# Loads of the later pairs moved to SyncE's queue in single rows, and two more pairs transposed by the DMA crossbar

## The chip, the cores and the metric

The kernel runs on one core of a Trainium2 chip. A core has a matrix engine (TensorE, PE in the profile, with its weight loads as PEld), a vector engine (VectorE, DVE), an engine for activation functions (ScalarE, ACT), a general one (GpSimd, POOL) and one that only waits and issues transfers (SyncE, SP). The transfers of all of them run on the same 16 DMA engines. The metric is the device time of one execution in microseconds (us), lower is better; several runs of the same kernel are given by their median.

## The reference

Two computations follow each other. The first is a gated linear recurrence: for each of 4 batches and 8 heads, with 768 positions t and a head size of 48,

```
state = alpha[t, :, None] * state + k[t] (outer) v[t]
y[t]  = q[t] @ state
```

The second is a two-layer network on y, read as x of 3072 rows (batch and position) by 384 (heads and their elements):

```
h   = x @ w_in            # 384 -> 2048
out = gelu_tanh(h) @ w_out  # 2048 -> 384, out is 3072 x 384 f32
```

All inputs are f32 in memory, laid out batch, head, position, element, so one head's row of one position is 48 x 4 = 192 bytes.

## The kernel before

**Tiles.** The 768 positions are cut into 6 chunks c of 128, and the 4 batches into 2 halves i. A "pair" m is one (c, i), numbered 0 to 11 with i running fastest: two units (batches) of one chunk, 128 positions by 2 batches by 8 heads by 48. Pairs 6 and 7 are chunk 3, pairs 8 to 11 are chunks 4 and 5.

**One pair.** `load` (L213) brings a strip of each of alpha (tile `a`), q, k in f32 (384 KB) and of v, cast to bf16 on the way (192 KB written). `ln` (L239, ACT) takes the logarithm of alpha, `cum` (L246, PE) sums it over positions with a triangular matrix, `exp` (L261, ACT) makes the decay b, its inverse, and the chunk's end decay. `scaled` (L276, DVE) makes q' = q b and k' = k / b (tiles `qp`, `kp`). q' and k' must then be transposed to have the head's elements on the partitions (tile `qkT`). There are two ways of doing this: `turn` and `turned` (L284, L301) with PE, 8 transposes a unit, into PSUM, and a copy out by DVE; or `turn_dma` (L308), a DMA transpose issued by SP, one for q' and one for k' of the whole pair. `attn` (L318) multiplies k' and q' per head, `mask` (L330, DVE) zeroes the upper part, `kv` (L338) and `carry` (L349) advance the state, `y` (L365) adds the state's part and the chunk's own part, `x` (L380) copies y to bf16, and x is transposed into `xT`, again by PE (`turn_x`, `turned_x`) or by SP (`turn_x_dma`, L315).

**One block** of the network is one pair's 256 rows: `layer1` (L396, 16 tiles of 3 matmuls) makes hT, `gelu` (L405, ACT) makes gT, `layer2` (L409) makes acc, `result` copies it to `ot`, and `store` (L424) sends it out through SP.

**Order.** Nothing is ordered by the hardware's own choice. `Scheduler.order` (L50) plays the kernel through on a clock of its own, with a cost for each task (the table `W`, L15), and gives each engine a fixed list. A task can start when its dependencies are done and when the buffer it takes (`BUFS`, L147) has been given back; of the tasks that could start within 60 ns of the earliest on an engine, the one with the lowest priority number goes first. A pair's tasks have numbers near 100 m; the network's tasks have 10000 and up, keep their own order, and fill what the pairs leave. ACT needs one table for ln and exp and another for gelu, so `DECAYS` (L139) says after which block's gelus each pair's ln and exp stand: those of pairs 6 and 7 both stand after block 4.

**Buffers that matter here.** Four each of `a`, `q`, `k` and six of `v`; one PSUM slot shared by `cum` and `at`; two (`yk`) shared by the PE transposes, kv, y and PE's transposes of x; four (`ff`) shared by hT and acc; four `qkT`; six `ot`.

**Queues.** In the kernel before, SP issues the first strip of alpha, all stores, and the DMA transposes, which pairs 8 to 11 use for q', k' (`TURN_QK`) and x (`TURN_X`, L146). POOL issues all other loads, in the order of `LOADS` (L143). Both issue strictly in order, and a transfer whose semaphore is not there yet holds all that stands behind it. A DMA of either queue also reuses the completion semaphore of the eighth before it on that queue, and waits for it.

Of the kernel before, what the change touches and what calls it, by code (L numbers as in the profile page):

```python
# [5 lines left out]
BF16 = mybir.dt.bfloat16  # L6
F16 = mybir.dt.float16
F32 = mybir.dt.float32
# [3 lines left out]
LN_EXP, GELU = 6, 0  # L12


W = dict(  # L15
    ln=760, exp=720, bend=170, gelu4=510, gelu2=340, table=1290,
    cum=530, t8=450, t4=225, attn=340, kv=170, inter=170, intra=205, tx=168, l1_4=655, l1_2=340, l2=655,
    qk2=910, qk1=500, ev8=650, ev4=350, mask=640, st=1400, st0=700, xc=520, xe=330, ot=540,
    ev8_act=960, ev4_act=520, xc_act=450, xe_act=450, ot_act=450,
    strip=2120, cast=1500, weight=1850, dma=2100, issue=1100, wissue=760, sp=100, store=2600, turn=1250, landed=2200, xbar_qk=1500, xbar_x=1000, first=3470, cold=500, fill=216, zero=1100,  # L20
)
LAT = {"SP": 0, "PE": 210, "ACT": 110, "DVE": 90, "POOL": 0}

# [1 line left out]
class Task:  # L25


    def __init__(self, kind, cost, prio, emit, deps=(), table=None, land=None, stream=None, xbar=0, late=0):
        self.kind, self.cost, self.prio, self.emit = kind, cost, prio, emit
        self.deps, self.takes = list(deps), []  # L30
        self.table, self.land, self.stream, self.xbar = table, land, stream, xbar
        self.late = late
        self.end = self.done = None

    def take(self, tag, *users):
# [4 lines left out]
class Scheduler:  # L40
# [9 lines left out]
    def order(self):  # L50
        free = {e: 0 for e in LAT}
        taken = {tag: [] for tag in self.bufs}
        table, wire, xbar, head, out = LN_EXP, 0, 0, 0, []
        left = {e: sorted((t for t in self.tasks if e in t.cost), key=lambda t: t.prio) for e in LAT}

        def given(tag):

            n, at = len(taken[tag]) - self.bufs[tag], 0
            for u in taken[tag][n] if n >= 0 else ():
                if u.done is None:  # L60
                    return None
                at = max(at, u.done)
            return at

        def ready(t):
            if t.stream not in (None, head):
                return None
            at = 0
            for d in t.deps:
                if d.done is None:  # L70
                    return None
                at = max(at, d.done)
            for tag, _ in t.takes:
                g = given(tag)
                if g is None:
                    return None
                at = max(at, g)
            return at

        def put(t, at, e):  # L80
            nonlocal wire, xbar
            for tag, users in t.takes:
                taken[tag].append(users)
            t.start, t.end, t.engine, t.load = at, at + t.cost[e], e, None
            free[e] = t.end
            t.done = t.end + LAT[e]
            if t.land is not None:
                wire = t.done = max(wire, t.end + W["dma"] - t.land) + t.land
            if t.kind in ("turn", "store"):
                xbar = t.done = max(xbar, t.end + W["landed"] - t.xbar) + t.xbar  # L90
                t.done += t.late
            out.append(t)

        while any(left.values()):
            best = None
            for e in LAT:
                found = []
                for t in left[e]:
                    at = ready(t)
                    if at is not None:  # L100
                        turn = W["table"] if t.table not in (None, table) else 0
                        at = max(at, free[e] + turn)
                        found.append((at, t, at - turn))
                if found:
                    window = min(f[2] for f in found) + 60
                    at, t, _ = min((f for f in found if f[2] <= window), key=lambda f: (f[1].prio, f[0]))
                    if best is None or at < best[0]:
                        best = at, e, t
            assert best is not None, "no task can go on"
            at, e, t = best  # L110
            if e == "PE" and self.fill and at < self.until and at - free[e] > 500:
                g = given("ff")
                n = int((at - max(free[e], g if g is not None else at) - 100) * 0.8 // W["fill"])
                if not free[e]:
                    n = int((at - W["zero"]) // W["cold"])
                if n > 0:
                    f = Task("fill", {"PE": n * W["fill"]}, 0, self.fill(n))
                    put(f.take("ff", f), max(free[e], g), e)
            put(t, at, e)
            if t.stream is not None:  # L120
                head += 1
            if t.table not in (None, table):
                table = t.load = t.table
            for q in t.cost:
                left[q].remove(t)
        return out
# [9 lines left out]
class _Kernel:  # L136
# [6 lines left out]
    LOADS = ("0", "1", "in 0", "in 1", "in 2", "in 3", "out 0", "out 1", "out 2", "out 3",  # L143
             "2", "3", "4", "5", "6", "7", "8", "9", "10", "11")

    TURN_QK, TURN_X = (8, 9, 10, 11), (8, 9, 10, 11)  # L146
    BUFS = dict(ca=1, yk=2, ff=4, la=3, qp=4, kp=4, b8=2, qkT=4, atm=6, x=3, ot=6, bend=8,  # L147
                a=4, q=4, k=4, v=6)

# [63 lines left out]
    def load(self, n, c, i, lo=0, hi=2):  # L213

        nc, C, H, D = self.nc, self.C, self.H, self.D
        u = self.p[c, i]

        def emit(e):
            if n not in u:
                u[n] = self.tile(n, [C, 2, H, D], BF16 if n == "v" else F32)  # L220
            src = self.src[n][2 * i + lo:2 * i + hi].rearrange("b h s d -> s (b h) d")[c * C:(c + 1) * C]
            (nc.sync if e == "SP" else nc.gpsimd).dma_start(u[n][:, lo:hi].rearrange("t b h d -> t (b h) d"), src)  # L222
        return emit

    def load_w(self, which, part):
# [203 lines left out]
    def tasks(self):  # L429
        s = self.s = Scheduler(self.BUFS, self.fill, 60000)  # L430
# [3 lines left out]
        pairs = list(self.p)  # L434


        loads, n = {}, 0

        def load(key, cost, emit):
            nonlocal n  # L440
            land = W[{"v": "cast", "w": "weight"}.get(key[0], "strip")]
            loads[key] = s.add("load", {"POOL": cost}, n, emit, land=land // 2 if key[0] != "w" and key[1] in self.SPLIT else land)
            n += 1

        def rows(m, names="aqkv"):
            for lo, hi in self.parts(m):
                for r in names:
                    load((r, m, lo), W["issue"] * (hi - lo) // 2, self.load(r, *pairs[m], lo, hi))
                    loads[r, m, hi - 1] = loads[r, m, lo]
# [6 lines left out]
        for step in self.LOADS:  # L456
            if step == "0":
                rows(0, "qkv")
            elif step.isdigit():
                rows(int(step))  # L460
            else:
                weights(*step.split())


        states, ys, xts, lns, ends = {}, {}, {}, {}, {}
        for m, (c, i) in enumerate(pairs):
            u, P = self.p[c, i], 100 * m
# [3 lines left out]
            for lo, hi in self.parts(m):  # L471
                n = hi - lo
# [10 lines left out]
                step = 1 if early else n  # L483
# [7 lines left out]
            exps[0].take("b8", *qp, *kp)  # L491
            vs, kvs, tq, cs, users = [], [], [], [], []
            if m in self.TURN_QK:
                tq = [s.add("turn", {"SP": W["turn"]}, P + 10, self.turn_dma(u, n), d, xbar=W["xbar_qk"]) for n, d in (("q", qp), ("k", kp))]
                owner, turned = tq[0], tq
            for j in range(2):
                b, o = 2 * i + j, P + 10 + 3 * j
                k = kp[j]
# [18 lines left out]
                          ms + turned + [loads["v", m, j]] + ([states[b, c - 1]] if c else []))  # L517
                xc = s.add("x", {"ACT": W["xc_act"], "DVE": W["xc"]}, P + 20 + j, self.x(u, j), [y])
                if m in self.TURN_X:
                    xe = tx = s.add("turn", {"SP": W["turn"]}, P + 22 + j, self.turn_x_dma(u, j, c, b), [xc], xbar=W["xbar_x"])  # L520
                else:
                    tx = s.add("tx", {"PE": W["tx"]}, P + 22 + j, self.turn_x(u, j), [xc])
                    xe = s.add("xe", {"DVE": W["xe"]}, P + 22 + j, self.turned_x(u, j, c, b), [tx])
                    tx.take("yk", xe)
# [4 lines left out]
                xts[c, b], ys[b, c] = xe, y  # L529
                vs.append(y)  # L530
                if c < NCH - 1:
                    kv = s.add("kv", {"PE": W["kv"]}, P + 30 + j, self.kv(u, j), [k, loads["v", m, j]])
                    st = states[b, c] = s.add("st", {"DVE": W["st" if c else "st0"]}, P + 30 + j, self.carry(u, j, c, b),
                                              [kv, be[j]] + ([states[b, c - 1], ys[b, c - 1]] if c else []))
                    kv.take("yk", st)
                    vs.append(kv)
                    kvs.append(kv)
                    cs.append(st)
# [106 lines left out]
```

## Time and profile before

| what | us |
|---|---|
| median of 3 runs | 188.83 (188.6 to 188.84) |
| the profiled execution, its own time | 188.71 |
| span of the profile | 186.9 |
| PE busy | 176.7 |
| ACT busy | 131.8 |
| DVE busy | 104.0 |
| POOL busy | 63.8 |

The span runs from the first to the last instruction of the profile; 1.8 us of the profiled execution's time lie outside it. Busy times are unions of instructions, so an engine that is 95% busy can only be passed by work that makes it shorter. Of the views, the page gives the shares, the chain that ended last gives what each stretch waited for, the stage table gives the busy time of each engine between two moments, the timelines give single instructions with the idle time before them in brackets, and the list of DMA issues gives the time from an issue to its landing.

### The profile page before, as it was taken

The page shows a single profiled execution, that of the slowest core. Times are in us where ns is not written, and L with a number is a line of the kernel's source. Part 1 is how long each engine was busy: PE and PEld are TensorE (multiplying, and loading weights), DVE is VectorE, ACT ScalarE, POOL GpSimd, SP SyncE. Part 2 cuts the span into 40 slices and gives each one's busy share as a digit, 9 for nine tenths or more (in the row PEclk, how much of TensorE's full clock was granted, in tenths as well). Part 3 has the DMA queues.
Part 4 walks back from the last instruction along what each step waited for, and adds up shares of the span by engine and source line. Part 5 has one row for each costly group of instructions (what it writes and reads, how often), then busy time and mean ns, then how long its engine had stood idle before and what let it go on. Part 6 is the DMA issues. An engine that isn't in the chain of part 4 may idle for free.

```text
span 186.9 us, 4504 instructions
## 1 busy us (share of the span) xinstructions
PE 176.7 (95%) x1831; PEld 127.2 (68%) x1834; DVE 104.0 (56%) x219; ACT 131.8 (71%) x297; POOL 63.8 (34%) x67
## 2 busy tenths in 40 slices
PE   5788899999999999999999999999999999999990
PEld 1344688666687687687688778667687687786850
DVE  7268670079787597497499798696644615000000
ACT  2544889853769769859799759788789884582911
POOL 7993443796456575566552200000000000000000
PEclk9999999999999999999999999999999999999999
DMA  6999999999999999999999997153270280301111
GB/s 131 174 183 169 206 204 212 200 178 229 240 217 186 151 227 205 175 231 200 180 218 222 186 207 136 43 123 76 46 178 22 49 190 14 101 15 47 42 42 44
DMA packets 49781, 27.56 MB, mean 147 GB/s; under 512 B 39744, under 2 KB 46400, under 8 KB 49760
## 3 DMA queue, kind: packets, MB, share of 16 engines
q0 software_dynamic: 32464, 19.27, 74.4%
q1 hardware_dynamic: 17296, 8.00, 17.5%
q8 instruction: 14, 0.23, 0.6%
q14 instruction: 7, 0.06, 0.1%
HBM read 25.17 MB, written 4.72 MB: 160 GB/s over the span
## 4 chain that ended last, share of the span: by engine, by line
PE 88%; ACT 4%; DVE 3%; DMA 2%; issue 1%
PE hT L400 34%; PE acc L414 34%; PE at L327 4%; PE qkT_ps L291 4%; PE cum L254 3%; PE yps L376 2%; DMA a<-in_alpha_dram 2%; PE yps L373 2%; PE kv L344 2%; PE idle L209 2%; PE xT_ps L390 1%; DVE atm L334 1%; ACT qkT L305 1%; PE cum L256 1%; DVE qp L280 1%
## 5 line engine op out<-in xcount | busy, mean ns | idle before, releaser
L406 ACT ACTIVATE gT<-hT 128x256 bf16<-128x256 f32 x192 | 63.5, 386 | 11.0 <-PE hT L400 10.5
L400 PE MATMUL hT<-xT,w_in 128*128 128x256 bf16 x576 | 69.9, 273 | 0.3 <-ACT gT L406 0.2
L414 PE MATMUL acc<-w_out,gT 128*128 128x384 bf16 x384 | 68.6, 326 | 0.0
L400 PEld LDWEIGHTS <-w_in 128*128 128x128 bf16 x576 | 54.2, 98 | 8.6 <-issue 0.8
L414 PEld LDWEIGHTS <-gT 128*128 128x128 bf16 x384 | 35.7, 97 | 20.4
L334 DVE TENSOR_TENSOR atm<-at,ut 128x512 bf16<-128x512 f32 x48 | 31.0, 686 | 13.8 <-PE at L327 12.9
L280 DVE TENSOR_TENSOR qp<-q,b 128x768 bf16<-128x768 f32 (+1 forms) x13 | 11.6, 892 | 19.0 <-ACT b L272 16.7
L421 ACT COPY ot<-acc 128x384 f32<-128x384 f32 x17 | 8.2, 480 | 18.7 <-PE acc L414 18.5
L222 POOL DMA_DIRECT2D k<-in_k_dram x13 | 14.5, 1113 | 12.3 <-DVE kp L280 6.0
L222 POOL DMA_DIRECT2D q<-in_q_dram x13 | 14.6, 1122 | 9.5 <-DMA q<-in_q_dram 3.0
L222 POOL DMA_DIRECT2D v<-in_v_dram x13 | 14.4, 1111 | 7.3 <-DMA a<-in_alpha_dram 2.7
L222 POOL DMA_DIRECT2D a<-in_alpha_dram x12 | 13.3, 1110 | 7.8 <-DMA k<-in_k_dram 1.9
L272 ACT ACTIVATE b<-cum 128x768 bf16<-128x768 f32 (+1 forms) x13 | 9.9, 762 | 7.7 <-PE cum L256 7.6
L243 ACT ACTIVATE la<-a 128x768 f16<-128x768 f32 (+1 forms) x13 | 10.2, 793 | 3.5 <-DMA a<-in_alpha_dram 3.3
L209 PE MATMUL idle<-zero 128*128 128x512 bf16 x31 | 11.2, 483 | 1.4 <-DVE zero L596 1.2
L361 DVE TENSOR_TENSOR st<-stmp,bend 64x192 bf16<-64x192 f32 x32 | 11.3, 353 | 1.7
L200 ACT ACT_TABLE_LOAD x9 | 11.5, 1283 | 0.9 <-PEq L629 0.7
L280 DVE TENSOR_TENSOR kp<-k,binv 128x768 bf16<-128x768 f32 (+1 forms) x15 | 11.7, 792 | 0.2 <-DMA k<-in_k_dram 0.2
L359 DVE TENSOR_TENSOR stmp<-kv,st 64x192 f32<-64x192 f32 x32 | 11.3, 352 | 0.9 <-PE kv L344 0.6
L406 ACT ACT_TABLE_LOAD x9 | 11.5, 1283 | 0.2
L305 DVE COPY qkT<-qkT_ps 128x1024 bf16<-128x1024 bf16 (+1 forms) x14 | 8.8, 649 | 4.7 <-PE qkT_ps L291 4.6
L383 DVE CAST x<-yps 128x384 bf16<-128x384 f32 x12 | 6.7, 556 | 7.6 <-PE yps L376 7.5
(43 smaller groups left out, 151.3 us busy)
## 6 DMA issues: line engine op xcount, KB each, us to landing
out_dram<-ot SPq DMA_DIRECT2D x24, 192.0 KB, 3.8
q<-in_q_dram POOLq DMA_DIRECT2D x11, 384.0 KB, 13.2
k<-in_k_dram POOLq DMA_DIRECT2D x11, 384.0 KB, 13.2
a<-in_alpha_dram POOLq DMA_DIRECT2D x10, 384.0 KB, 13.0
v<-in_v_dram POOLq DMA_DIRECT2D x11, 192.0 KB, 13.0
w_in<-in_moe_w_in_dram POOLq DMA_DIRECT2D x4, 384.0 KB, 11.8
w_out<-in_moe_w_out_dram POOLq DMA_DIRECT2D x4, 384.0 KB, 15.3
a<-in_alpha_dram SPq DMA_DIRECT2D x1, 384.0 KB, 4.2
```

The lines of the kernel that those rows point to most:

```text
L200: nc.scalar.add_instruction(mybir.InstLoadActFuncSet(name=nc.get_next_instruction_name(), act_func_set_id=i, engine=mybir.EngineType.Activ ...
L209: self.nc.tensor.matmul(ps, self.zero[:, 0:self.C], self.zero, start=True, stop=True)
L222: (nc.sync if e == "SP" else nc.gpsimd).dma_start(u[n][:, lo:hi].rearrange("t b h d -> t (b h) d"), src)
L243: self.nc.scalar.activation(u["la"][:, lo:hi, :, 0:self.D], u["a"][:, lo:hi], AF.Ln)
L280: self.nc.vector.tensor_tensor(u[n + "p"][:, lo:hi, :, 0:self.D], u[n][:, lo:hi], u["b" if n == "q" else "binv"][:, lo:hi], op=ALU.mult)
L305: self.copy(e)(t, u.pop(("T_ps", i, which)))
L334: self.nc.vector.tensor_tensor(u["atm", i][:, o], u["at", i][:, o], self.ut[:, None, :].to_broadcast([self.C, self.H // 2, self.C]), op=AL ...
L359: nc.vector.tensor_tensor(s[ps], acc, old[ps, :, fs], op=ALU.add)
L361: nc.vector.tensor_tensor(new[ps, :, fs], acc, u["bend"][ps, i, :, None].to_broadcast([64, H // 2, D]), op=ALU.mult)
L400: self.nc.tensor.matmul(h, self.w_in[:, j, nt * self.C:(nt + 1) * self.C], self.xT[c][:, j, lo:hi].rearrange("p g t -> p (g t)"), start=j ...
L406: return lambda e: self.nc.scalar.activation(self.gT[c % self.NG][:, nt, lo * self.C:hi * self.C], f.pop(("h", c, lo, nt)), AF.Gelu_apprx_ ...
L414: self.nc.tensor.matmul(f["acc", c, b], self.gT[c % self.NG][:, nt, b * self.C:(b + 1) * self.C], self.w_out[:, nt, :], start=nt == 0, sto ...
```

## The change

The diff does five things.

1. From pair 4 on (`ON_SP`), the strips of a, q and k are issued by SP, with a priority of 100 m + 5, instead of by POOL. The access pattern is the same; v stays with POOL, since it is cast.
2. A new POOL task, `hold`, copies one element. Before SP's first strip it reads k of pair 3 and writes into the new tile of a, so that SP's strips start only when k of pair 3 has landed. Before each v from pair 4 on it reads k of the same pair and writes into the tile of v, so that each v is issued only when its k has landed.
3. `TURN_QK` takes in pairs 6 and 7: their q' and k' are transposed by the crossbar, no longer by PE with a copy by DVE.
4. In the scheduler's clock, SP becomes one server: a strip costs 2750 ns, a store 650, a transpose of q' or k' 1350, of x 600, and a transfer of SP counts as landed 2200 ns after its end. The separate clock of the crossbar is gone.
5. `kv` waits, in the scheduler's clock, for the state and the y of the chunk before. In the program nothing is added by that but the place of kv in PE's list.

```diff
-    strip=2120, ..., sp=100, store=2600, turn=1250, landed=2200, xbar_qk=1500, xbar_x=1000, ...
+    strip=2120, ..., sp=650, landed=2200, xbar_qk=1350, xbar_x=600, row=2750, ...
...
-            if t.kind in ("turn", "store"):
-                xbar = t.done = max(xbar, t.end + W["landed"] - t.xbar) + t.xbar
-                t.done += t.late
+            if e == "SP" and t.land is None:
+                t.done += W["landed"]
...
-    TURN_QK, TURN_X = (8, 9, 10, 11), (8, 9, 10, 11)
+    ON_SP = 4
+
+    TURN_QK, TURN_X = (6, 7, 8, 9, 10, 11), (8, 9, 10, 11)
...
+    def hold(self, m, n, m1, n1):
+        pairs = list(self.p)
+        u, last = self.p[pairs[m]], self.p[pairs[m1]]
+
+        def emit(e):
+            u[n] = self.tile(n, [self.C, 2, self.H, self.D], BF16 if n == "v" else F32)
+            self.nc.gpsimd.tensor_copy(u[n][:, 0, 0, 0:1], last[n1][:, 0, 0, 0:1])
+        return emit
...
+            if key[0] in "aqk" and key[1] >= self.ON_SP:
+                loads[key] = s.add("load", {"SP": W["row"]}, 100 * key[1] + 5, emit, [gate])
+                n += 1
+                return
+            deps = []
+            if key[0] == "v" and key[1] >= self.ON_SP:
+                deps = [s.add("gate", {"POOL": 100}, n, self.hold(key[1], "v", key[1], "k"), [loads["k", key[1], 0]])]
...
+                if int(step) == self.ON_SP:
+                    gate = s.add("gate", {"POOL": 100}, n, self.hold(int(step), "a", int(step) - 1, "k"), [loads["k", int(step) - 1, 0]])
...
-                tq = [s.add("turn", {"SP": W["turn"]}, P + 10, self.turn_dma(u, n), d, xbar=W["xbar_qk"]) for n, d in (("q", qp), ("k", kp))]
+                tq = [s.add("turn", {"SP": W["xbar_qk"]}, P + 10, self.turn_dma(u, n), d) for n, d in (("q", qp), ("k", kp))]
...
-                    xe = tx = s.add("turn", {"SP": W["turn"]}, P + 22 + j, self.turn_x_dma(u, j, c, b), [xc], xbar=W["xbar_x"])
+                    xe = tx = s.add("turn", {"SP": W["xbar_x"]}, P + 22 + j, self.turn_x_dma(u, j, c, b), [xc])
...
-                    kv = s.add("kv", {"PE": W["kv"]}, P + 30 + j, self.kv(u, j), [k, loads["v", m, j]])
+                    kv = s.add("kv", {"PE": W["kv"]}, P + 30 + j, self.kv(u, j), [k, loads["v", m, j]] + ([states[b, c - 1], ys[b, c - 1]] if c else []))
```

More of the change, by code (lines that the diff above doesn't have):

```diff
@@ L19 @@
     ev8_act=960, ev4_act=520, xc_act=450, xe_act=450, ot_act=450,
-    strip=2120, cast=1500, weight=1850, dma=2100, issue=1100, wissue=760, sp=100, store=2600, turn=1250, landed=2200, xbar_qk=1500, xbar_x=1000, first=3470, cold=500, fill=216, zero=1100,
+    strip=2120, cast=1500, weight=1850, dma=2100, issue=1100, wissue=760, sp=650, landed=2200, xbar_qk=1350, xbar_x=600, row=2750, first=3470, cold=500, fill=216, zero=1100,
 )
@@ L25, with __init__ @@
 class Task:
-    def __init__(self, kind, cost, prio, emit, deps=(), table=None, land=None, stream=None, xbar=0, late=0):
+    def __init__(self, kind, cost, prio, emit, deps=(), table=None, land=None, stream=None):
         self.kind, self.cost, self.prio, self.emit = kind, cost, prio, emit
         self.deps, self.takes = list(deps), []
-        self.table, self.land, self.stream, self.xbar = table, land, stream, xbar
-        self.late = late
+        self.table, self.land, self.stream = table, land, stream
         self.end = self.done = None
@@ L52, in order @@
         taken = {tag: [] for tag in self.bufs}
-        table, wire, xbar, head, out = LN_EXP, 0, 0, 0, []
+        table, wire, head, out = LN_EXP, 0, 0, []
         left = {e: sorted((t for t in self.tasks if e in t.cost), key=lambda t: t.prio) for e in LAT}
@@ L80, in put @@
         def put(t, at, e):
-            nonlocal wire, xbar
+            nonlocal wire
             for tag, users in t.takes:
@@ L434, in tasks @@
         pairs = list(self.p)
-        loads, n = {}, 0
+        loads, n, gate = {}, 0, None
         def load(key, cost, emit):
@@ L441, in load @@
             land = W[{"v": "cast", "w": "weight"}.get(key[0], "strip")]
-            loads[key] = s.add("load", {"POOL": cost}, n, emit, land=land // 2 if key[0] != "w" and key[1] in self.SPLIT else land)
+            if key[0] in "aqk" and key[1] >= self.ON_SP:
[5 more added lines that the diff above has]
+                deps = [s.add("gate", {"POOL": 100}, n, self.hold(key[1], "v", key[1], "k"), [loads["k", key[1], 0]])]
+            loads[key] = s.add("load", {"POOL": cost}, n, emit, deps, land=land // 2 if key[0] != "w" and key[1] in self.SPLIT else land)
             n += 1
```

## The prediction

> **What bounds the kernel now.** I read the page's busy shares and its chain first.
>
> ```profile
> span 186.9 us, 4504 instructions
> ...
> PE 176.7 (95%) x1831; PEld 127.2 (68%) x1834; DVE 104.0 (56%) x219; ACT 131.8 (71%) x297; POOL 63.8 (34%) x67
> ...
> PE 88%; ACT 4%; DVE 3%; DMA 2%; issue 1%
> ```
>
> PE is idle for 186.9 - 176.7 = 10.2 us, nearly all at the two ends. The stage table, which has the time and then the busy time of PE, PEld, DVE, ACT and POOL, confirms it for the stages around the change:
>
> ```profile
> 78.80:93.40 14.60, 14.60 (x173) 11.06 (x172) 10.08 (x21) 11.61 (x26) 9.17 (x8) 1.00 1.38 203
> 93.40:109.30 15.90, 15.90 (x195) 12.27 (x193) 14.31 (x31) 13.15 (x28) 4.65 (x5) 1.00 1.18 206
> 109.30:125.30 16.00, 15.82 (x185) 11.78 (x184) 13.22 (x26) 12.64 (x28) 0.00 (x0) 1.00 0.50 113
> ```
>
> PE has no gap from 78.8 to 109.3 us. So only PE work that goes away can gain, and any wait put into PE's list is paid. Next, what the transposes of pairs 6 and 7 take of the chain in order of time (start, duration):
>
> ```profile
> 93.45 0.89 PE qkT_ps L291 x16
> ...
> 103.82 0.45 PE qkT_ps L291 x8
> 104.51 0.18 PE cum L254
> 104.77 0.47 PE qkT_ps L291 x8
> ```
>
> Then ACT's timeline where it goes from exp back to gelu for blocks 5 and 6:
>
> ```profile
> 94.41 1.28 ACT L406 ACT_TABLE_LOAD   x1
> 95.71 2.45 ACT L406 ACTIVATE gT<-hT 128x256 bf16<-128x256 f32 x8
> ...
> 106.79 1.28 ACT L406 ACT_TABLE_LOAD   x1
> 109.63 1.82 ACT L406 ACTIVATE gT<-hT 128x256 bf16<-128x256 f32 x5 [1.56 <-PE hT L400]
> ```
>
> The first gelu of block 5 follows its table load at once: ACT isn't waiting for PE there. The first gelu of block 6 has waited 1.56 us for PE. This decides below what each pair's transposes are worth. Last, the transfers: from the lists of issues for 36 to 62 us and for 121 to 160 us (the last number is us to landing), from the queue shares at 1.8 to 4.1 us (packets, MB), and from POOL's timeline:
>
> ```profile
> out_dram<-ot SPq DMA_DIRECT2D x4, 192.0 KB, 8.1
> ...
> out_dram<-ot SPq DMA_DIRECT2D x5, 192.0 KB, 2.1
> qkT<-qp SPq DMA_TRANSPOSE x3, 3.2
> ...
> q1 hardware_dynamic: 2064, 0.39, 87.2%
> ...
> 48.73 1.15 POOL L222 DMA_DIRECT2D q<-in_q_dram  x1 [1.08 <-DMA k<-in_k_dram]
> ```
>
> SP's store takes four times as long beside POOL's loads. SP's one strip, the first alpha, moved its 0.39 MB in 2064 packets within that 2.3 us window, 4.2 us from issue to landing. POOL's wait of 1.08 us ends as k of pair 3 lands: the place of the new gate, about 48.7 us.
>
> **What the Trainium skill says.** "DMA: Bandwidth & Descriptors", section "Queues, rings and completion order", says that each DMA engine takes turns between queues packet by packet, a whole packet at a time. The 8.1 against 2.1 us agrees: POOL's strips go in few large packets, a store gets one packet in between. The same page's "Specifications" asks for 512 B a transfer for full rate; the 192 B rows still made 0.39 MB / 2.3 us = 170 GB/s here, against some 200 GB/s in the stage table. Its "Rules for kernel authors" says that a transpose beside ordinary DMAs needs no serializing, so the transposes add no wait for strips; no run shows one beside rows yet.
>
> **The change part by part.**
>
> *Transposes removed.* Pair 6: 0.89 us on the chain; pair 7: 0.45 + 0.47 = 0.92. Together 1.81 us of PE. DVE loses four copies of 0.69 us (the page's L305 row has 649 ns mean over two forms); DVE has idle time before the masks and isn't the bound, so nothing.
>
> *Pair 7.* Its k' is made at 101.47 + 0.96 = 102.4 us (DVE's timeline), and its first `at` stands at 107.53 on the chain, 5.1 us later. The DMA path is 3.2 us from issue to landing. It fits with 1.9 us to spare, and ACT has 1.56 us of room. I take the whole 0.92 us.
>
> *Pair 6.* k' ends at 92.05 + 0.95 = 93.0 us. By PE and the copy the first `at` starts at 95.0, 2.0 us later; by DMA not before 93.0 + 3.2 = 96.2, 1.2 us later. What can PE do from 93.45 on? kv (0.45 us) and four hT tiles of 0.33 us (1.3 us, all that `ff` holds until a gelu has run): to 95.2. The first gelu ends at 95.71 + 0.39 = 96.1. So PE waits about 0.9 us: what the transposes took, ACT's pinned start gives back. It is pinned because exp of pair 6, cum of pair 7 and exp of pair 7 follow each other through one PSUM slot. The bounds are 0.89 us gained (other work moves up) and 1.2 us lost (at late, nothing moves up); I take 0.
>
> *Strips on SP.* POOL loses 24 issues of 1.15 us; it is at 34%, nothing. For supply: the gate at 48.7; first packets 1.1 us after an issue (0.74 to about 1.85); so 49.9, plus the 2.3 us of that window for a strip and some 0.9 us to the landing (4.2 - 1.1 - 2.3): a, q, k of pair 4 land by about 53, 55.5 and 58. They are used at 59.90, 62.91 and 63.79 (ln and DVE). Afterwards a pair wants about 14 us, and three strips take 8.3 us at 2.75 us each (the change's own figure, which the 2.3 us of the trace plus a third of a v supports). Supply runs ahead until the four buffers hold it. Cost: nothing; for pair 4 the cover is 6 to 7 us, for later pairs more.
>
> *v behind its k.* v of pair 4 is issued at about 58 and lands 5.8 us later if as quick as the shortest v of the trace, at 64; 13 us like the median was the depth of a full queue, which is gone. kv of pair 4 is at 66.81. Nothing, with 2.8 us of cover.
>
> *SP's order.* SP gains 24 strips (0.45 us issue in the one case) and 4 transposes (1.24 and 1.29 us). Behind an instruction that waits stand stores, strips and transposes of others; stores have six `ot` at two per 14 us, strips have the cover above. Only transposes are waited for soon. A strip ahead in the ring delays one by up to 2.3 to 2.75 us, but the list puts transposes (610, 710) ahead of later strips, and the list's clock counts the strip. What it doesn't count is v on POOL's queue taking turns: a whole v took 1.3 to 1.9 us between landings in POOL's timeline, so 0 to 1.9 us per pair of transposes. v moves some 1.6 of every 8.3 us, a fifth of the time, so 0.4 us on average, of which the list's 3.55 us for a landing of 3.2 covers 0.35. I take 0.1 us for pair 6; pair 7 covers its own.
>
> *kv's place, stores and x at other costs in the list.* No instruction changes. Nothing, bounded at 0.5 us either way from the 0.18 us that stage 109.3 to 125.3 leaves idle and from small reorderings.
>
> **Sum:** 0.92 (pair 7) + 0 (pair 6) - 0.1 (v beside it) = 0.8 us gained. The profiled execution, 188.71 = 186.9 + 1.8, would become 187.9; the median of the runs, 0.12 us above it, 188.0.
>
> **Rivals.**
>
> A, the forecast, 188.0 (own range 187.4 to 188.45): 43%.
>
> B, all 1.81 us are gained: PE's list moves hT or cum so that pair 6 doesn't wait. 188.83 - 1.8 = 187.0. For it: a full PE everywhere; against: ACT's start at 95.71. 11%.
>
> C, nothing is left: the wait of pair 6 becomes the full 1.2 us and contention takes the rest. 0.92 gained less 1.2 is a loss of 0.3, and the 0.5 us of reordering goes either way: 188.45 to 189.2, middle 188.8. 14%.
>
> D, slower: the crossbar's transposes land late in PE's fixed list. PE reaches `at` of pair 6 where the list's clock had it landed (1.35 + 2.2 = 3.55 us after SP begins), and the whole PE queue, hT included, stands behind it. For it: stores beside loads were 8.1 instead of 2.1 us, and a transpose's packets take turns with v's. Against: rows are small packets and stand in SP's own ring. At half of a store's excess, (8.1 - 2.1) / 2 = 3.0 us, pair 6 loses 3.0 us, pair 7 3.0 - 1.9 = 1.1, against 0.92 gained: +3.2, 192.0; at a quarter of it, 1.5 - 0.9 = +0.6, 189.4. It decides from a lateness of 0.9 us on pair 6. I put its middle at 190. 28%.
>
> E, supply: strips at over 3.7 us (from 49.9, three and a 5.8 us v by 66.8) make kv of pair 4 late, and a strip at 5 us gives +4 us, 192.8. Against it stands 2.3 us. 4%.
>
> **How the numbers follow.** Faster by over 0.2% (0.38 us, about what a measurement of this kernel can tell from no change) is A and B: 0.54. Within it is C: 0.14. Slower is D and E: 0.32. The range of 187.0 to 190.9 leaves out half of B, a third of D (beyond 2 us of loss) and E: about 2 in 10.
>
> **What would show it.** Right: L291 with 16 fewer for each of qp and kp, chain pieces of PE without qkT_ps at pairs 6 and 7; transposes of q' and k' at 3 to 4 us to landing, all 12; a small PE wait before the first gelu of block 5 and none at pair 7; SP strips at 2.0 to 2.8 us apart. Wrong: `at` of pairs 6 or 7 waiting for DMA qkT by over 1 us, transposes over 5 us to landing, ln or q' waiting for a, q; or a new order that leaves PE idle elsewhere.

## The result and the profile after

The changed kernel took 193.25 to 198.15 us in four runs, median 195.05, against 188.84 beside it: slower, by a ratio of 1.0297 with an interval of 1.0207 to 1.0386. (The ratio leaves out the run at 198.15 us, in which TensorE's clock was lowest.) The forecast was 188.0, its range ended at 190.9.

From the page of the changed kernel, the profiled execution of 194.21 us:

```profile
span 192.4 us, 4454 instructions
...
PE 175.9 (91%) x1802; PEld 125.2 (65%) x1802; DVE 100.8 (52%) x213; ACT 133.1 (69%) x299; POOL 39.2 (20%) x52
...
PE 62%; DMA 20%; POOL 6%; DVE 4%; ACT 3%; issue 3%; SPq 0%; POOLq 0%; DVEq 0%
...
q<-in_q_dram SPq DMA_DIRECT2D x8, 384.0 KB, 6.1
```

PE's busy time fell by 0.8 us, all of it in the first 60 us, where no transpose was moved; its idle time grew from 10.2 to 192.4 - 175.9 = 16.5 us. Of the chain's 20% DMA, 7% is `qkT<-kp`; most of the rest are loads in the first 40 us, where the chain now runs another way, though PE is no later (the same 18 hT matmuls start at 84.5 us in both). A strip of q takes 6.1 us from issue to landing, not the 4.2 of the one that ran alone. The stage table of the changed kernel (time; busy PE, PEld, DVE, ACT, POOL; TensorE's clock; DMA share; GB/s) and its PE timeline, where only lines from 60 us on with over 1 us of idle time before them are copied, say where PE stood; the last fence has the stage from 125.3 us in the kernel before:

```profile
78.80:93.40 14.60, 14.60 (x174) 11.06 (x172) 10.04 (x21) 11.61 (x26) 2.09 (x3) 1.00 1.40 187
93.40:109.30 15.90, 14.81 (x173) 11.00 (x170) 14.21 (x30) 12.36 (x29) 1.43 (x2) 1.00 1.37 167
109.30:125.30 16.00, 14.19 (x170) 10.31 (x167) 9.75 (x21) 12.86 (x27) 2.60 (x4) 1.00 1.19 160
125.30:137.20 11.90, 9.59 (x78) 6.75 (x76) 4.58 (x12) 7.71 (x19) 0.76 (x1) 0.87 1.34 193
```

```profile
96.11 2.45 PE L410 MATMUL hT<-xT,w_in 128*128 128x256 bf16 x21 [1.04 <-ACT gT L416]
...
114.49 0.40 PE L337 MATMUL at<-qkT 64*128 64x128 bf16 x8 [1.63 <-DMA qkT<-kp]
...
133.77 0.44 PE L337 MATMUL at<-qkT 64*128 64x128 bf16 x8 [2.31 <-DMA qkT<-kp]
...
146.62 0.40 PE L337 MATMUL at<-qkT 64*128 64x128 bf16 x8 [1.18 <-DMA qkT<-kp]
```

```profile
125.30:137.20 11.90, 11.90 (x132) 8.59 (x132) 8.12 (x16) 9.87 (x22) 0.00 (x0) 1.00 0.36 84
```

Until 93.4 us PE is as full as before. The first wait, 1.04 us before hT of block 5, is the one that the prediction placed at pair 6. The other three are waits of `at` for the transposed k', and they are not those of pairs 6 and 7, which the change moved to the crossbar, but of pairs 8, 9 and 10, which were there already and had no such wait before.

A second cost stands in the chain in order of time of the changed kernel:

```profile
124.36 0.95 DVE kp L290
...
128.69 5.04 DMA qkT<-kp
133.77 0.44 PE at L337 x8
134.21 3.64 PE acc L424 x12
...
188.97 0.48 ACT ot L431
```

Twelve acc matmuls take 1.95 us elsewhere in the same chain; here, after the longest wait, 3.64. TensorE ran at half its clock, the 0.87 of the last stage line: 1.69 us more. The sum is then: waits 1.04 + 1.63 + 2.31 + 1.18 = 6.16 us, clock 1.69, removed PE transposes -1.81, together +6.0. The last copy of `ot`, at 188.97 us here, stands in the chain of the kernel before at

```profile
182.76 0.48 ACT ot L421
```

so that up to there 6.2 us were lost, which the sum nearly explains. The span grew by 192.4 - 186.9 = 5.5 only, because from this copy to the end it is 4.1 us in the kernel before and 3.4 here. This end, in which the network has no work left, is shorter by 0.5 to 0.7 us in the profiles of e2, e5, e6, e7 and e8 too (not in e12); why was not looked into, and a gain in it says nothing for strips or transposes.

Why the transposes were late is seen in SP's timeline of the changed kernel and in the list of its issues from 92 to 160 us:

```profile
118.98 3.96 SPq L326 DMA_TRANSPOSE xT<-x  x2
123.00 1.54 SPq L222 DMA_DIRECT2D a<-in_alpha_dram  x1
124.67 1.61 SPq L436 DMA_DIRECT2D out_dram<-ot  x1
126.39 1.34 SPq L320 DMA_TRANSPOSE qkT<-qp  x1
128.23 0.40 SPq L436 DMA_DIRECT2D out_dram<-ot  x1
128.69 2.08 SPq L320 DMA_TRANSPOSE qkT<-kp  x1
130.81 0.57 SPq L222 DMA_DIRECT2D q<-in_q_dram  x1
```

```profile
v<-in_v_dram POOLq DMA_DIRECT2D x4, 192.0 KB, 6.3
qkT<-qp SPq DMA_TRANSPOSE x6, 4.6
qkT<-kp SPq DMA_TRANSPOSE x6, 4.1
xT<-x SPq DMA_TRANSPOSE x6, 4.0
```

These are pair 9's transposes. Ahead of them stand two transposes of x, alpha of pair 11 and a store; between them another store; and v of pair 10 moves on POOL's queue from 124.9 to 130.9. k' was ready at 124.36 + 0.95 = 125.3 us, but SP issued its transpose only at 128.69, so 3.4 us passed before the issue. Landings were 6.1 and 5.0 us after the issues, where the kernel before had 3.1 for both. In the kernel before the last k landed at 112.8 us, so that the crossbar, first used at 111.7, found the DMA engines almost free. Now the last k lands at 137.8.

What shared the DMA engines with the transposes differs from pair to pair. The queue shares (packets, MB; q1 is SP's queue, q0 POOL's) from 108.6 to 114.0 us, the time of pair 8's transposes, and from 141.6 to 146.57, the time of pair 10's, are:

```profile
q1 hardware_dynamic: 3151, 0.94, 120.3%
```

```profile
q1 hardware_dynamic: 2694, 0.83, 96.1%
q0 software_dynamic: 1370, 0.13, 66.2%
```

Pair 8's landed after 5.0 and 4.5 us, and until 114.0 us no packet of v was beside them; ahead of them in SP's own queue were k of pair 9, which landed at 110.8, and a store. So SP's own queue is enough to make a transpose late. Pair 10's landed after 4.1 and 3.6 us, beside v and behind a transpose of x and a store, but with no strip left. Pair 9 had both, a strip and v.

### The profile page after: what moved, and what is told of

Read it like the earlier page. It is cut to its first block, busy times and chain, and to the rows that moved or that the text cites. A ratio compares the mean times of both kernels' runs of the same rounds, so it can differ in the third digit from the quotient of the medians.

```text
span 192.4 us, 4454 instructions
## 1 busy us (share of the span) xinstructions
PE 175.9 (91%) x1802; PEld 125.2 (65%) x1802; DVE 100.8 (52%) x213; ACT 133.1 (69%) x299; POOL 39.2 (20%) x52
## 4 chain that ended last, share of the span: by engine, by line
PE 62%; DMA 20%; POOL 6%; DVE 4%; ACT 3%; issue 3%; SPq 0%; POOLq 0%; DVEq 0%
PE acc L424 27%; PE hT L410 22%; DMA w_out<-in_moe_w_out_dram 8%; DMA qkT<-kp 7%; DMA a<-in_alpha_dram 5%; PE at L337 3%; PE cum L264 2%; PE qkT_ps L301 2%; ACT b L282 2%; PE yps L386 2%; PE yps L383 2%; POOL w_in L240 2%; POOL v L222 1%; POOL k L222 1%; PE kv L354 1%
## 5 line engine op out<-in xcount | busy, mean ns | idle before, releaser
L424 PE MATMUL acc<-w_out,gT 128*128 128x384 bf16 x384 | 70.3, 331 | 0.0
L410 PEld LDWEIGHTS <-w_in 128*128 128x128 bf16 x576 | 54.1, 98 | 10.2 <-issue 2.0
L424 PEld LDWEIGHTS <-gT 128*128 128x128 bf16 x384 | 36.2, 99 | 21.5 <-issue 1.9
L232 POOL CAST v<-k 128x1 bf16<-128x1 f32 x8 | 2.8, 351 | 75.4 <-DMA k<-in_k_dram 42.2
L337 PE MATMUL at<-qkT 64*128 64x128 bf16 x192 | 9.6, 219 | 5.6 <-DMA qkT<-kp 5.1
L253 ACT ACTIVATE la<-a 128x768 f16<-128x768 f32 (+1 forms) x13 | 10.2, 793 | 5.7 <-DMA a<-in_alpha_dram 5.6
L337 PEld LDWEIGHTS <-qkT 64*128 64x128 bf16 x192 | 5.4, 94 | 11.5 <-DMA qkT<-kp 6.1
L393 DVE CAST x<-yps 128x384 bf16<-128x384 f32 x11 | 6.1, 557 | 11.2 <-PE yps L386 11.2
L209 PE MATMUL idle<-zero 128*128 128x512 bf16 x34 | 10.2, 423 | 1.2 <-DVE zero L615 1.2
L282 ACT ACTIVATE binv<-cum 128x768 bf16<-128x768 f32 (+1 forms) x13 | 9.8, 755 | 0.0
```

Of the source, the lines that this page charges most:

```text
L209: self.nc.tensor.matmul(ps, self.zero[:, 0:self.C], self.zero, start=True, stop=True)
L282: self.nc.scalar.activation(u[n].rearrange("t i h d -> t i (h d)")[:, lo:hi], u["cum"][:, lo:hi, 0:H * D], AF.Exp, scale=1.0 if n == "b" e ...
L337: nc.tensor.matmul(at[:, o, p, :], t[sl, 1, p, :], t[sl, 0, p, :], start=True, stop=True)
L410: self.nc.tensor.matmul(h, self.w_in[:, j, nt * self.C:(nt + 1) * self.C], self.xT[c][:, j, lo:hi].rearrange("p g t -> p (g t)"), start=j ...
L424: self.nc.tensor.matmul(f["acc", c, b], self.gT[c % self.NG][:, nt, b * self.C:(b + 1) * self.C], self.w_out[:, nt, :], start=nt == 0, sto ...
```

## Experiments

The kernel before, run beside each, had 188.62 to 188.71 us; ratios are to it.

**e1, no late strips.** From the changed kernel; strips of pairs 9 to 11 are left out:

```diff
         def emit(e):
+            if e == "SP" and 2 * c + i >= 9:
+                u[n] = self.p[c - 2, i][n]
+                return
             if n not in u:
```

> The changed kernel, but the strips of a, q and k of pairs 9, 10 and 11 are left out: these pairs compute on the strips of two chunks before, all else and every engine's order stays. Theory Q (queue): the transposes of pairs 8, 9 and 10 are late because they stand in SP's ring behind strips and stores that in the kernel before had gone by 113 us. Then they land in 3.1 to 3.6 us, PE's waits for them (1.63, 2.31 and 1.18 us) and the halved clock go, the wait of 1.0 us at pair 6 stays: 188.83 - 1.8 + 1.0 = 188.0, 187.3 to 188.8. Rival P (plan): the new order of cum, exp and masks itself leaves PE without work, and the transposes only end the wait: the waits stay under another name, over 191. Rival S (supply): not tested apart, it too would gain.

Measured: 190.13 us (189.15 to 192.75), ratio 1.0083 (1.0058 to 1.0108): 4 us of the loss are gone, but the range of 187.3 to 188.8 was missed. The waits at pairs 8 and 9 are gone and the one at pair 10 is down to 0.33 us; their transposes land in 3.0 to 3.2 us. One came up elsewhere, at pair 6:

```profile
100.28 0.40 PE L340 MATMUL at<-qkT 64*128 64x128 bf16 x8 [1.63 <-DMA qkT<-kp]
```

With the strips gone the v's of pairs 9 to 11 no longer wait for a k that has still to land, so they all moved between 95 and 109 us, beside the transposes of pairs 6 and 7, which landed after up to 5.7 and 9.4 us. So the list itself isn't the cause (rival P falls), but strips are not the only thing that delays a transpose.

**e2, strips only**, and **e12, the list only.** From the changed kernel, and e12 with `ON_SP = 12` besides, so that no load is on SP:

```diff
-    TURN_QK, TURN_X = (6, 7, 8, 9, 10, 11), (8, 9, 10, 11)
+    TURN_QK, TURN_X = (8, 9, 10, 11), (8, 9, 10, 11)
```

> The strips on SP and v behind k as in the change, but pairs 6 and 7 transposed by PE as before. Theory Q: the strips of pairs 10 and 11 still share the ring with the transposes of pairs 8 and 9, with four transposes (5.4 us of ring time) fewer ahead of them; PE's waits at pairs 8 to 10 shrink to 1 to 4 us in sum, no 1.0 us at pair 6: 189.5 to 192.5. Rival T67: the four added transposes are what overfills SP; without them 188.4 to 189.2, as before.

> Only the two edits of the list's clock (other costs of SP's work, kv later in PE's list); all loads on POOL and the crossbar for pairs 8 to 11 as in the kernel before. The strips alone gave a span 0.5 us shorter in their profile. If that came from the list, this gives 188.1 to 188.4; if from the strips, 188.5 to 188.9.

Measured: e2 188.79 us (188.13 to 192.51), ratio 1.0014 (0.9993 to 1.0035); e12 188.72, ratio 1.0002 (0.9994 to 1.0011). So the list's costs and kv's place did nothing, and moving the strips alone is on average not slower: my expectation of 189.5 to 192.5 was wrong for the median, and rival T67 held. But e2's runs fall into two groups: eleven of 20 took 188.13 to 188.94 us, nine 189.67 to 192.51, which is the range that I had expected. The trace is of the first group, so what the nine waited for isn't shown. In this trace PE is through with its work when it is in the kernel before (last copy of `ot` at 182.71 us); its span is 0.5 us shorter at the end alone. The last k landed at 125.0 us. Pair 8's transposes landed late there as well (5.7 and 5.8 us), but PE had other work; no wait of PE from 60 us on exceeds 0.2 us.

**e3, transposes only.** The kernel before with `TURN_QK = (6, 7, 8, 9, 10, 11)`.

> The kernel before, with all loads on POOL, but pairs 6 and 7 transposed by the crossbar. Theory Q with turns taken packet by packet: a store of 8 packets an engine landed 3 to 7 us late beside POOL's strips; a transpose has 64 an engine, so its landing takes 20 us or more while POOL's queue is full (until 113 us): pair 6's at waits 10 us or more, 198 to 215. Rival (bytes decide, not packets): transposes land in 5 to 9 us, PE waits 2 to 6 us in sum, 189 to 193.

Measured: 216.41 us, ratio 1.1434 (1.1387 to 1.148), just above the range for turns by the packet and far from the rival's 189 to 193. The PE timeline of the profiled execution, which took 220.06 us:

```profile
127.52 0.61 PE L327 MATMUL at<-qkT 64*128 64x128 bf16 x8 [30.18 <-DMA qkT<-kp]
```

One wait is nearly the whole loss of 31 us in it. q' of pair 6 landed 19.8 us and k' 33.4 us after the issue: beside POOL's strips, which go mostly in packets of 4224 bytes in this trace, a transpose in packets of 256 bytes hardly moves. The Trainium skill ("DMA: Bandwidth & Descriptors", section "Queues, rings and completion order") says that turns between queues are taken by the packet, and this agrees. It also shows what the strips on SP are good for: with them the same transposes landed in 3.3 to 4.2 us at pair 6 (in the changed kernel).

**e4, transposes later in the list.** From the changed kernel:

```diff
-                t.done += W["landed"]
+                t.done += W["landed"] + (2000 if t.kind == "turn" and t.prio < 1200 else 0)
```

> The changed kernel, but the list's clock counts the transposes of q', k' and x as landed 2000 ns later, so that PE's list has other work before each at. Theory Q with the list as the place where it bites: waits of PE for the transposes fall under 0.5 us each, the clock stays whole, and the list's own longer plan (1.6 us on its clock) is what remains: 189.0 to 191.0. Rival P or a plain lack of room on the ring: the waits come back or other idle time takes their place, 192.5 or more.

Measured: 190.28 us (190.05 to 191.05), ratio 1.0087 (1.0065 to 1.0109). The waits for transposes shrank to 0.70 and 0.87 us, which is more than the 0.5 expected, the clock stayed whole, and 1.04, 0.37 and 0.36 us of PE idle time came from ACT and the masks. Of the 3.0% (5.6 us) that the changed kernel lost, 0.9% (1.6 us) is left. So some 4.0 us of the loss come from the list, which put `at` at a landing (3.55 us) that the chip didn't keep. What is left wasn't taken apart.

**e5, no late v**, and **e6, neither late v nor late strips.** e5 from the changed kernel, with v of pairs 8 to 11 left out; e6 is e5 with e1's edit.

```diff
+            if n == "v" and 2 * c + i >= 8:
+                return
...
+            if n == "v" and m >= 8:
+                u[n] = self.p[pairs[m - 6]][n]
+                return
```

> The changed kernel, but v of pairs 8 to 11 isn't loaded (they use v of three chunks before, and the gate of v goes too); all strips stay, and all orders but POOL's. Theory Q-strips: strips and stores ahead in SP's own ring make the transposes late, so the three waits of PE stay at 1 us or more each: 192 or more. Theory Q-v: v's packets on POOL's queue, which take turns with the transposes', make them late: the waits at pairs 9 and 10, whose transposes ran beside v, fall under 0.5 us, the one at pair 8, whose transposes landed before v's first packet, stays: 189.5 to 191.5.

> The changed kernel without both: v of pairs 8 to 11 and the strips of a, q, k of pairs 9 to 11 are left out, old ones are used. If the queue is all that made it slow (strips and v together), transposes land in 3.1 to 4.3 us, PE's only wait is the 1.0 us at pair 6, and 1.8 us of PE work is gone: 188.0, 187.5 to 188.5. If the list itself costs, 189 or more.

Measured: e5 187.89 us (187.7 to 188.03), ratio 0.9956 (0.9943 to 0.9969); e6 188.11 (187.57 to 188.67), ratio 0.997 (0.9957 to 0.9982). With all strips still on SP, e5's issues and its only waits of PE after 60 us (0.17 us of another left out) are:

```profile
qkT<-qp SPq DMA_TRANSPOSE x6, 3.2
qkT<-kp SPq DMA_TRANSPOSE x6, 3.1
```

```profile
96.19 2.45 PE L415 MATMUL hT<-xT,w_in 128*128 128x256 bf16 x21 [1.04 <-ACT gT L421]
...
140.11 0.40 PE L342 MATMUL at<-qkT 64*128 64x128 bf16 x8 [0.29 <-DMA qkT<-kp]
```

That is the forecast's account of PE: -1.8 of work, +1.0 at pair 6, and 0.3 more. The last copy of `ot` stands at 182.46 us in e5 and at 182.51 in e6, against 182.76 before: the transposes gained 0.3 us there, and the other 0.7 and 0.6 us of the shorter spans lie in the end behind it. Even pair 8's wait went, whose transposes in the changed kernel ran when no v moved, so my reading that only a v in the same moment counts was too narrow: without v of pair 8 the strips and transposes ahead ran earlier too (k of pair 9 landed at 108.2 instead of 110.8 us). Taking away the strips as well gains nothing more.

**e7, only pair 7 added.** The changed kernel with `TURN_QK = (7, 8, 9, 10, 11)`.

> The change with pair 7 added to the crossbar but pair 6 left on PE. By the terms of the prediction pair 7 gives 0.92 us and has no wait at ACT's start: 187.8. By theory Q its two transposes put 2.7 us more on a ring that strips only just clear by 125 us (188.79 with the strips alone): a wait of PE of 0 to 2 us at pairs 8 and 9, 188.2 to 190.5, with a wide spread.

Measured: 188.39 us (187.83 to 188.92), ratio 0.9987 (0.9979 to 0.9994). This is the low end of theory Q's 188.2 to 190.5, without its wide spread. In the profiled execution (188.49) PE waited 0.32, 1.01 and 0.17 us for transposes, more than the 0.92 us of work that pair 7 saved.

**e9 and e10, v ahead.** From the changed kernel; e10 also with pair 6 on PE.

```diff
+                g = {4: 4, 5: 5, 6: 5, 7: 5, 8: 6, 9: 6, 10: 7, 11: 7}[key[1]]
-                deps = [s.add("gate", {"POOL": 100}, n, self.hold(key[1], "v", key[1], "k"), [loads["k", key[1], 0]])]
+                deps = [s.add("gate", {"POOL": 100}, n, self.hold(key[1], "v", g, "k"), [loads["k", g, 0]])]
```

> The changed kernel with all its loads, but v waits for the k of an earlier pair: v of pairs 5, 6, 7 behind k of pair 5, 8 and 9 behind 6, 10 and 11 behind 7, so that v is through before the crossbar's transposes begin at 92 us. All lists but POOL's stay. Theory Q-v: v beside the transposes is what made them late; they land as without v (3.1 to 4.9 us), PE's waits at pairs 8 to 10 go: 188.0, 187.6 to 189.0. Rival (bytes): it is the whole load on the DMA engines, and v moved forward makes the strips of pairs 6 to 9 as much later, which then meet the transposes: 190 to 194. Against both stands that strips of pair 6 may be late for ln (88 us).

> The same early v, and only pair 7 added to the crossbar, pair 6 on PE. Theory Q-v: the 1.0 us before pair 6's hT isn't there, 0.92 us of PE work is gone and no transposes are late: 187.8 (the best execution with v behind its k had 187.83), and the spread narrows. Rival (bytes): as with v behind its k, 188.4, or slower.

Measured: e9 195.8 us (195.09 to 196.14), ratio 1.0373 (1.0351 to 1.0396); e10 193.51 (191.43 to 194.35), ratio 1.0208 (1.0136 to 1.028). In e9 the waits at pairs 8 to 10 did go, all but 0.25 us (their transposes landed in 3.1 to 3.7 us, with the strips still in SP's queue), and pair 6 paid for them. Its PE timeline and, for 92 to 107 us, its stage line:

```profile
104.29 0.61 PE L337 MATMUL at<-qkT 64*128 64x128 bf16 x8 [5.72 <-DMA qkT<-kp]
```

```profile
92.00:107.00 15.00, 8.24 (x81) 6.33 (x80) 8.05 (x18) 6.58 (x17) 2.66 (x4) 0.87 1.61 195
```

The last v landed at 103.4 instead of 144.6 us, but k of pair 7 landed at 91.1 instead of 85.9 and k of pair 8 at 97.9 instead of 94.4, so these met the transposes of pair 6, which were issued 3 us later and landed 7 us after their issue. So theory Q-v was right about pairs 8 to 10, and the rival (bytes) about the whole: v moved forward delays the strips, and these meet the transposes. Even the rival's 190 to 194 was too low for e9. In e10 the first transposes, those of pair 7, pay with a wait of 3.26 us.

**e11, v ahead and x of pair 7 on the crossbar**: `TURN_X = (7, 8, 9, 10, 11)` added to e9.

> Early v, pairs 6 and 7 on the crossbar as in the change, and x of pair 7 on it too. If the gain that x of pair 7 gave the kernel before (188.62 to 187.37) adds to the change with early v: 186.7 to 187.3. If the crossbar's list is then so full that transposes hold each other: 188 to 190.

Measured: 196.11 us (194.81 to 197.3), ratio 1.0393 (1.0341 to 1.0445): as e9, with a wait of 5.36 us at pair 6, and outside both ranges.

**e8, x of pair 7 on the crossbar, on the kernel before.**

```diff
-    TURN_QK, TURN_X = (8, 9, 10, 11), (8, 9, 10, 11)
+    TURN_QK, TURN_X = (8, 9, 10, 11), (7, 8, 9, 10, 11)
```

> The kernel before, all loads on POOL, with one more use of the crossbar: x of pair 7, made at about 112 to 114 us, when POOL's queue has just emptied (112.8). PE loses two groups of 0.17 us: 188.83 - 0.34 = 188.4 to 188.5. Rival: on SP's list these two stand between the transposes of pair 8's q' and k' and hold them, or xT lands late for block 7: 188.8 to 190.

Measured: 187.37 us (187.33 to 187.61), ratio 0.9932 (0.992 to 0.9944): the fastest of all. Its issues from 105 to 121 us:

```profile
xT<-x SPq DMA_TRANSPOSE x2, 2.4
qkT<-qp SPq DMA_TRANSPOSE x1, 3.7
qkT<-kp SPq DMA_TRANSPOSE x1, 3.1
```

The two new transposes were issued at 113.3 and 114.5 us, as POOL's last k landed (113.8), and they land as quickly as other transposes of x with no load beside them (2.3 us). The gain, 1.25 us, is more than the 188.4 to 188.5 forecast: the last copy of `ot` stands 0.8 us earlier (181.98), of which 0.34 us are PE transposes and 0.17 us a wait before hT of block 7 that also went, with 0.3 us open; the other 0.5 us lie in the end behind it.

## Why the prediction was wrong

**What held.** The bound (PE), the price of the transposes (1.81 us), the wait of about 0.9 us at pair 6 behind ACT's gelus (1.04, in the changed kernel and, the same, in e1, e5 and e6), pair 7 without such a wait, the supply of pair 4 (predicted landings 53, 55.5 and 58 us, v at 64; measured 53.6, 55.6, 58.1 and 63.2), and the list's edits at nothing (e12). That e5 and e6 came to the forecast (187.89 and 188.11, against 188.0) is in part luck: the transposes gained 0.3 us in them, not 0.8, and the shorter end, which the prediction didn't have, made up for it.

**The step that failed** is "SP's order", with its term of 0.1 us for pair 6. In its place stand 5.1 us of waits for transposes at pairs 8 to 10 and 1.69 us of half clock. The step asked for the delay of the four added transposes alone. Those of pairs 8 to 10 were not costed at all, because the kernel before showed them at 3.2 us; but it showed them on DMA engines that the loads had just left. It also held that the transposes add no wait for strips: with four more of them the last k landed at 137.8 us, without these four (e2) at 125.0. The step before it, "Supply runs ahead until the four buffers hold it", had the figures to see this: at 8.3 us a pair from 48.7 us, five pairs are in by about 91, and three pairs remain for the time of the crossbar. Measured, k of pair 8 landed at 94.4 us, near enough to that. I compared these times with when the strips are needed, found cover of many microseconds, and never asked what shares SP's queue and the DMA engines with them. From there strips, v, and 12 instead of 8 transposes of 256 KB moved together; SP's fixed order, in which each transfer is issued after the one before it (alpha of pair 11 at 123.0 us, behind two transposes of x that held SP for 3.96 us), pushed the strips out further.

**Rival D was the mechanism, at another place.** It had the transposes late in PE's fixed list, but at pairs 6 and 7. The waits of 1.63, 2.31 and 1.18 us were at pairs 8, 9 and 10. Its price for a lateness of 1.5 us each (189.4) counts one wait, since pair 7 had cover; in the runs there were three without cover, and the clock.

**The clock was not in the prediction.** It cost 1.69 us in the profiled execution. The loss doesn't hang on it: the execution of 193.25 us had the whole clock. That of 198.15 us had the lowest, 0.983 on average, so the clock may be part of the spread; that was not tested apart.

**What is the cause, and what isn't settled.** Shown: it takes both parts. The strips alone are neutral in the median (e2; nine of 20 runs were 1 to 4 us slower), the transposes alone cost 28 us (e3), together 6. Shown also: less load on the DMA engines in the crossbar's time removes the waits for transposes, all but 0.3 and 0.5 us (e5, e6), another order of the same load only moves them (e9, e10), and a list that expects the delay saves most, but not all (e4). Shown too: what stands ahead in SP's own queue can delay a transpose (the packets at pair 8), and v on POOL's queue can (pair 7 in e1, 9.4 us with no strip left). Not settled is how the delay of pair 9 divides between the two and SP's late issue; taking away either was enough for pairs 8 and 9. Not settled either is what e2's slower runs waited for.

## What to carry to other kernels

A transfer's latency is a property of the queues at that moment: k' of pair 6 landed 3.2 us after its issue in e5 and 33.4 us after it in e3. When a change puts latency-critical transfers on a queue, list everything else that the queue and the DMA engines will carry at that time, the old transfers included, and not only those that the change adds; a latency read in an idle stretch is a lower bound. Here small critical transfers placed after the bulk came through without delay (e8), and a fixed list that allowed for a late landing saved most of the loss (e4). Where a change in a profile lies matters too: up to 0.7 us of some spans here came and went behind the last work.

## What the runs showed of the hardware

- **Half clock with waits of 2.3 us and more.** In the profiled executions, PE waits of up to 1.63 us left the clock whole (the changed kernel at pair 8, e1). With 2.31 us (pair 9), 3.26 us (e10), 5.36 us (e11) and 5.72 us (e9) it was halved, for 3.4, 3.4, 3.4 and 6.8 us by the trace's clock records. At pair 9 the half clock began at 134.0 us, and in the 3.4 us before that PE had been idle for 2.31. The Trainium skill ("TensorE: Matmul & The Clock Gate", section "Part 1: The HAM clock gate") says that the clock falls after an idle window of some 3.4 us and that the windows run freely. The lengths agree with it; the wait that was enough was shorter than a window here.
- **Single rows moved fewer bytes a second than packed strips in the same stage.** The stage tables of 64 to 78 us have, in the kernel before and in the changed one (last number GB/s):

```profile
64.00:78.00 14.00, 14.00 (x161) 10.64 (x160) 9.88 (x21) 11.20 (x25) 8.43 (x8) 1.00 1.64 198
```

```profile
64.00:78.00 14.00, 14.00 (x161) 10.64 (x160) 9.88 (x21) 11.20 (x25) 2.06 (x3) 1.00 1.24 167
```

  PE's work is the same to the instruction. The DMA share fell as well, from 1.64 to 1.24, so the rows may not have been held up by the DMA engines alone; SP also stands at stores until `ot` is there. How much each does, the runs don't tell.
- **Loads on two queues took from each other.** e9 moved v of pairs 6 to 11 earlier on POOL's queue, and k on SP's queue became 5.2 us (pair 7) and 3.5 us (pair 8) later. The skill's "DMA: Bandwidth & Descriptors", section "Issuing engines are not separate DMA queues", says that transfers of all issuing engines run on the same 16 DMA engines and interleave, which agrees.
